# A fixed least time per DMA packet in the scheduler's picture, and row normalisation for the GEGLU layers begun one step ahead of its finish

## The chip, the cores and the metric

The kernel runs on one core of a Trainium2 chip. The metric is the device time of one execution in microseconds; for the kernel before the change three runs gave a median of 1600.6 us. Engines are named as the profile names them: PE (matmuls), PEld (its weight loads), DVE (elementwise), ACT (activations), POOL (GpSimd), SP (which issues most of the DMAs). "SPq" and "POOLq" are DMA issues on those queues.

## The reference, cut to what matters

The input is one sequence of 2048 rows with 512 columns in float32. Four layers alternate: a Fourier mixing layer (matrices for the hidden and the sequence direction, real part kept) and a GEGLU layer of width 1792. Each layer normalises the rows first and adds its result to the row.

```
def _A_ref(x, dft_seq_re, dft_seq_im, dft_hid_re, dft_hid_im):
    a = jnp.einsum("bsd,ed->bse", x, dft_hid_re)
    b = jnp.einsum("bsd,ed->bse", x, dft_hid_im)
    return jnp.einsum("ts,bse->bte", dft_seq_re, a) - jnp.einsum("ts,bse->bte", dft_seq_im, b)

def _B_ref(x, w_gate, w_up, w_down):
    return (_gelu(x @ w_gate) * (x @ w_up)) @ w_down

x = A_x
x = x + _A_ref(_layernorm(x, axis=-1), A_dft_seq_re, A_dft_seq_im, A_dft_hid_re, A_dft_hid_im)
x = x + _B_ref(_layernorm(x, axis=-1), B_w_gate, B_w_up, B_w_down)
x = x + _A_ref(_layernorm(x, axis=-1), A_dft_seq_re, A_dft_seq_im, A_dft_hid_re, A_dft_hid_im)
x = x + _B_ref(_layernorm(x, axis=-1), B_w_gate, B_w_up, B_w_down)
```

## The kernel before, in words

**Products.** Every float32 operand is split into a high and a low part of a shorter format. ACT writes the high part as a rounded copy (L121), DVE the low part as source minus high part (L123). A product is then three matmuls (`mm3`: L161 high by high, L162 high by low, L163 low by high), each with 128x128 weights and 512 moving columns, accumulated in one of eight PSUM banks. Larger products are done by blocks with seven instead of eight block products (the names A11, S1 to S4, T1 to T4, B11 and so on), which costs sums and differences on DVE (L149, L152) and copies out of PSUM on ACT (L156).

**Stages.** The layers follow each other: mixing layer 0 (`mix`, four blocks of 512 rows), GEGLU layer 1 in two halves of 1024 rows (`geglu`, w = 0 and 1), mixing layer 2, GEGLU layer 3 in two halves. SBUF is handed out in 93 slots of 128x512 (`sb.get`, `sb.put`). Two larger tiles, `wide` and `xwide`, hold four slots' width each; `load_turned` brings a group of 512 rows into one of them by four DMAs whose pieces are 512 bytes long (L229).

**Rows for a GEGLU layer.** `block_steps` prepares 1024 normalised rows as eight tiles of 128 rows. For each tile `norm(i)` starts the loads of the tiles that come next (`x_load_mixed`, four DMAs of 64 KB, L198), normalises its own tile (`normed`), turns it in 32x32 squares into its quarter of `wide` (DVE, L624) and, after each fourth tile, stores `wide` to DRAM (POOL's queue, L627). Later `fetch` reads it back by columns (L638, pieces of 512 bytes).

**Normalisation.** For the layers after the first, `norm_terms` needs ACT, POOL and ACT again, in this order: sum of the row (L518), mean (L519), sum of squares (L520) on ACT; add and power on POOL (L521, L522); shift on ACT (L523). `normed` then writes the normalised tile on ACT (L540). ACT's two passes over the row (L518, L520) must write their 512 columns somewhere, though only the sums are used: in `normed` they go into the tile `z` that later takes the result, in `terms_ahead` (which makes only the two terms, for mixing layer 2) into the one tile `junk`.

**What sets the order.** Python writes the steps in one order: a list `queue` that gives a step after each product, a list `slow` of which every ninth step takes one (`PACE`), and `chores` spread over the products of a mixing layer. For the first half of the rows of a GEGLU layer the steps of `block_steps` are chores of the mixing layer; for the second half they are in `slow` during w = 0. Then a scheduler reorders the instructions of each engine by a simulated time. The numbers of that picture are set in `machine_as_traced`: among them 3000 ns for an SP DMA to start, and 21.5 bytes per ns for each DMA engine. Each engine executes its own list strictly in order, so an ACT instruction that waits holds all that stand behind it.

Of the kernel before, what the change touches and what calls it, by code (L numbers as in the profile page):

```python
# [9 lines left out]
F32 = mybir.dt.float32  # L10
# [4 lines left out]
P = 128  # L15
# [6 lines left out]
NT = TB // P  # L22
# [28 lines left out]
SP_DELAY_NS = 3000  # L51
DEPTH = 1
DMA_BYTES_PER_NS = 21.5


@with_exitstack
def fnet_geglu(ctx: ExitStack, tc: tile.TileContext, x_in, ws, wh, whc, wgu, wdc, out):
# [468 lines left out]
    def terms_ahead(layer, i, n):  # L526
# [6 lines left out]
        known[layer, i] = norm_terms(layer, i, x, junk)  # L533
        sb.put(x)

    def normed(layer, i, mixed=False):
        x = row_of(layer, i, mixed)
        z = sb.get()
        rstd, shift = known.pop((layer, i), None) or norm_terms(layer, i, x, z)
        nc.scalar.activation(z, x, AF.Identity, bias=shift, scale=rstd)  # L540
        sb.put(x)
        return z
# [63 lines left out]
    def block_steps(layer, w):  # L606

        zt, t, wide = {}, {}, {}
        turned = [dram.tile([P, NT * D], F32, name=f"t{layer}_{w}_{part}") for part in range(2)]

        def norm(i):

            def run():
                r0 = w * 2 * NT
                end = 2 * NT if w else i // NT * NT + NT
                for k in range(i if i == 0 or i + NT == end and not w else i + 2, min(i + 3, end)):
                    fresh["mixed", r0 + k] = x_load_mixed(layer, r0 + k)
                z = normed(layer, r0 + i, True)
                part, n = divmod(i, NT)
                if n == 0:  # L620
                    assert not sb.out("z")
                    wide[part] = tpool.tile([P, NT * D], F32, name="wide")
                to = wide[part].rearrange("p (b n t) -> p b n t", n=NT, t=32)
                nc.vector.transpose(to[:, :, n], z.rearrange("p (b t) -> p b t", t=32))  # L624
                sb.put(z)
                if n == NT - 1:
                    nc.gpsimd.dma_start(turned[part], wide.pop(part))  # L627
# [25 lines left out]

        def second(c):
            def run():
                v = zt.pop((c, 1))
                if c < 2:
                    t["B12", c] = v
                    t["T1", c] = difference(v, t["B11", c])
                    sb.put(t.pop(("B11", c)))  # L660
                else:
                    c0 = c - 2
                    t["T2", c0] = difference(v, t["T1", c0])
                    t["T3", c0] = difference(v, t["B12", c0])
                    sb.put(t.pop(("B12", c0)))
                    blocks["B22", c0] = split_slot(v)
                    sb.put(v)
            return run

        def fourth(c):  # L670
            def run():
                t["T4", c] = difference(t["B21", c], t["T2", c])
                sb.put(t.pop(("B21", c)))
            return run

        def divide(name, c):
            def run():
                blocks[name, c] = split_slot(t[name, c])
                sb.put(t.pop((name, c)))
            return run  # L680

        one = [norm(i) for i in range(2 * NT)]
        two = [fetch(c) for c in range(ND)] + [first(c) for c in range(ND)] + [second(c) for c in range(ND)]
        two += [fourth(c) for c in range(2)]
        two += [divide(name, c) for name in ("T2", "T3", "T1", "T4") for c in range(2)]
        return one, two
# [690 lines left out]
def machine_as_traced():  # L1377
# [1 line left out]
    from concourse import hw_specs  # L1379

    spec = hw_specs.TRN2Spec
    kept = {name: getattr(spec, name) for name in ("PE_FULL_CLOCK_PASS_GAP_NS", "DGE_DMA_DELAY", "ENG_ISSUE_QUEUE_DEPTH", "DMA_BUS_BYTES_PER_NS_PER_ENGINE")}
    spec.PE_FULL_CLOCK_PASS_GAP_NS = PASS_GAP_NS
    spec.DGE_DMA_DELAY = {**spec.DGE_DMA_DELAY, mybir.EngineType.SP: SP_DELAY_NS}
    spec.DMA_BUS_BYTES_PER_NS_PER_ENGINE = DMA_BYTES_PER_NS
    depth = {mybir.EngineType.DVE: DEPTH, mybir.EngineType.Activation: DEPTH}
    spec.ENG_ISSUE_QUEUE_DEPTH = {**spec.ENG_ISSUE_QUEUE_DEPTH, **depth}
    try:
# [51 lines left out]
```

## Time and profile before

| | |
|---|---|
| runs | 1600.6 us median (1600.12 to 1602.94, 3 runs) |
| the profiled execution | 1600.54 us |
| its span, first to last instruction | 1598.8 us |
| TensorE clock | 0.999 of full speed |
| busy | PE 1586.9 us, DVE 1236.8, ACT 856.4, POOL 225.2 |
| matmuls | 7026, in three groups of 2334 and 24 short ones ahead |

A line of the trace gives start, duration, engine, line of the kernel, operation, output and inputs (buffer numbers left out) and count; behind it, in brackets, stands how long the engine was idle before it and what ended that. A matmul's duration (0.39 us) is longer than the distance to the next one, since matmuls overlap; the distance is what counts.

### The profile page before, as it was taken

How to read it: one execution, taken by the hardware profiler on the slowest of the kernel's cores; microseconds unless marked ns; L12 is line 12 of the kernel's file. 1: busy time of each engine (PE TensorE's matmuls, PEld its weight loads, DVE VectorE, ACT ScalarE, POOL GpSimd, SP SyncE). 2: the span in 40 equal slices, each digit the busy share in tenths (PEclk: the TensorE clock that was granted, in tenths of full speed). 3: DMA queues.
4: the chain of work that ended last, by engine and by line, in shares of the span. 5: the costliest groups of instructions: out<-in, count | busy, mean ns of one | idle time of the engine just before them, and what ended most of it. 6: DMA issues, size and time to landing. Idle time of an engine off the chain costs nothing.

```text
span 1598.8 us, 23017 instructions
## 1 busy us (share of the span) xinstructions
PE 1586.9 (99%) x7026; PEld 1313.1 (82%) x7026; DVE 1236.8 (77%) x2148; ACT 856.4 (54%) x1680; POOL 225.2 (14%) x410
## 2 busy tenths in 40 slices
PE   9999999999999999999999999999999999999998
PEld 7888788888878888788888888888888888888887
DVE  8999879789789795665869988789985548754484
ACT  7864454545666653556777435436446545433361
POOL 2212200112465201220041000001001000000000
PEclk9999999999999999999999999999999999999999
DMA  9949987787989899995967677778998967897462
GB/s 362 329 158 331 352 273 254 234 285 265 339 321 332 296 311 308 292 363 180 305 229 247 239 267 244 251 248 240 266 328 237 293 207 234 295 257 227 133 191 54
DMA packets 276379, 422.85 MB, mean 264 GB/s; under 512 B 28864, under 2 KB 131264, under 8 KB 275232
## 3 DMA queue, kind: packets, MB, share of 16 engines
q1 hardware_dynamic: 251600, 338.26, 67.0%
q0 software_dynamic: 23840, 82.73, 14.1%
q8 instruction: 56, 0.92, 0.2%
q14 instruction: 67, 0.55, 0.1%
q10 hardware_dynamic: 816, 0.39, 0.1%
HBM read 339.74 MB, written 81.53 MB: 263 GB/s over the span
## 4 chain that ended last, share of the span: by engine, by line
PE 83%; issue 12%; DMA 3%; ACT 1%; POOL 1%; DVE 0%; SPq 0%; POOLq 0%; ACTq 0%; DVEq 0%
PE p L162 28%; PE p L161 28%; PE p L163 28%; DMA s<-ws 2%; POOL rstd L521 0%; DMA wide<-x 0%; DMA s<-x 0%; ACT s L121 0%; DMA s<-wdc 0%; SPq L293 0%; ACT s L540 0%; DVE s L123 0%; DVE s L152 0%; POOL out L242 0%; ACT s L156 0%
## 5 line engine op out<-in xcount | busy, mean ns | idle before, releaser
L162 PE MATMUL p<-s,s 128*128 128x512 f32 (+1 forms) x2334 | 903.2, 388 | 1.1 <-DVE s L123 1.1
L163 PE MATMUL p<-s,s 128*128 128x512 f32 (+1 forms) x2334 | 891.9, 388 | 0.0
L161 PE MATMUL p<-s,s 128*128 128x512 f32 (+1 forms) x2334 | 874.9, 388 | 2.0 <-ACT s L156 1.5
L121 ACT ACTIVATE s<-s 128x512 fp32r<-128x512 f32 (+1 forms) x834 | 467.6, 607 | 344.4 <-DVE s L149 125.3
L123 DVE TENSOR_TENSOR s<-s,s 128x512 fp32r<-128x512 f32 (+1 forms) x834 | 521.2, 660 | 56.1 <-ACT s L121 53.9
L161 PEld LDWEIGHTS p<-s,s 128*128 128x128 f32 x2334 | 438.2, 188 | 94.6 <-ACT s L121 2.4
L162 PEld LDWEIGHTS p<-s,s 128*128 128x128 f32 x2334 | 438.4, 188 | 92.4 <-DVE s L123 2.6
L163 PEld LDWEIGHTS p<-s,s 128*128 128x128 f32 x2334 | 438.2, 188 | 89.7
L152 DVE TENSOR_TENSOR s<-s,p 128x512 f32<-128x512 f32 x290 | 194.8, 682 | 197.8 <-PE p L163 114.1
L149 DVE TENSOR_TENSOR s<-s,s 128x512 f32<-128x512 f32 (+1 forms) x403 | 242.3, 617 | 7.2 <-DMA s<-ws 4.9
L156 ACT ACTIVATE s<-p 128x512 f32<-128x512 f32 x246 | 143.8, 592 | 142.2 <-PE p L163 141.3
L1035 ACT ACTIVATE s<-s 128x512 f32<-128x512 f32 x112 | 70.1, 629 | 120.8 <-DVE s L152 120.1
L521 POOL TENSOR_SCALAR rstd<-rstd 128x1 f32<-128x1 f32 x48 | 18.6, 387 | 356.7 <-ACT s L520 271.3
L1049 DVE TENSOR_TENSOR s<-s,s 128x512 f32<-128x512 f32 x84 | 57.8, 688 | 1.7
L276 POOL DMA_DIRECT2D wb<-s x84 | 45.5, 544 | 88.7 <-ACT s L121 64.0
L121 ACT ACTIVATE s<-xwide 128x512 fp32r<-128x512 f32 (+1 forms) x66 | 39.8, 615 | 27.8 <-DVE xwide L149 14.6
L152 DVE TENSOR_TENSOR s<-s,s 128x512 f32<-128x512 f32 (+1 forms) x69 | 40.2, 586 | 15.6 <-DMA s<-ws 6.1
L540 ACT ACTIVATE s<-s,shift,rstd 128x512 f32<-128x512 f32 x59 | 47.6, 810 | 4.6 <-DVE shift L512 4.0
L123 DVE TENSOR_TENSOR s<-xwide,s 128x512 fp32r<-128x512 f32 (+1 forms) x66 | 44.0, 673 | 4.0 <-ACT s L121 3.1
L242 POOL DMA_DIRECT2D out<-wide x8 | 5.2, 655 | 287.1 <-DVE wide L152 182.2
L242 POOL DMA_DIRECT2D x<-wide x12 | 7.8, 659 | 234.1 <-DVE wide L152 234.1
L624 DVE STREAM_TRANSPOSE wide<-s 128x512 f32<-128x512 f32 x31 | 21.8, 705 | 20.3 <-ACT s L540 17.6
(121 smaller groups left out, 520.7 us busy)
## 6 DMA issues: line engine op xcount, KB each, us to landing
s<-ws SPq DMA_DIRECT2D x361, 256.0 KB, 5.1
s<-wb SPq DMA_DIRECT2D x294, 256.0 KB, 5.5
s<-wc SPq DMA_DIRECT2D x196, 256.0 KB, 4.8
wb<-s POOLq DMA_DIRECT2D x98, 256.0 KB, 5.8
s<-wh SPq DMA_DIRECT2D x85, 256.0 KB, 5.0
xwide<-ws SPq DMA_DIRECT2D x55, 256.0 KB, 4.5
s<-x SPq DMA_DIRECT2D x54, 256.0 KB, 4.5
wc<-s POOLq DMA_DIRECT2D x49, 256.0 KB, 6.0
```

Of the source, the lines that this page charges most:

```text
L121: nc.scalar.activation(hi, src, AF.Copy)
L123: nc.vector.tensor_tensor(lo, src, f32(hi), op=ALU.subtract)
L149: nc.vector.tensor_tensor(out, a, b, op=ALU.subtract)
L152: nc.vector.tensor_tensor(out, a, b, op=ALU.add)
L156: nc.scalar.activation(v, src, AF.Copy)
L161: nc.tensor.matmul(ps, ah, bh, start=start, stop=False, skip_group_check=True)
L162: nc.tensor.matmul(ps, ah, bl, start=False, stop=False, skip_group_check=True)
L163: nc.tensor.matmul(ps, al, bh, start=False, stop=stop, skip_group_check=True)
L276: nc.gpsimd.dma_start(a, f32(t))
L540: nc.scalar.activation(z, x, AF.Identity, bias=shift, scale=rstd)
L1035: nc.scalar.activation(t, g, AF.Gelu_apprx_tanh)
L1049: nc.vector.tensor_tensor(t, t, v, op=ALU.mult)
```

## The change

Two things change. First, the scheduler's picture gets a least time of 37 ns for each DMA packet (`DMA_MIN_TRANSFER_TIME`), beside the 21.5 bytes per ns; nothing of this is in the program itself, only the order that comes out of it. Second, in `block_steps` a step `norm(i)` only begins its tile (`norm_begun`: load and `norm_terms`, with `junk` as scratch), and `turn(i - 1)` finishes the one before (scale, transpose, store). One more step at the end finishes the last tile. All other callers of `normed` begin and finish at once, with `junk` as scratch too.

```
+DMA_PACKET_NS = 37
...
+    begun = {}
+    def norm_begun(layer, i, mixed=False):
+        x = row_of(layer, i, mixed)
+        begun[layer, i] = x, known.pop((layer, i), None) or norm_terms(layer, i, x, junk)
     def normed(layer, i, mixed=False):
-        x = row_of(layer, i, mixed)
+        if (layer, i) not in begun:
+            norm_begun(layer, i, mixed)
+        x, (rstd, shift) = begun.pop((layer, i))
         z = sb.get()
-        rstd, shift = known.pop((layer, i), None) or norm_terms(layer, i, x, z)
         nc.scalar.activation(z, x, AF.Identity, bias=shift, scale=rstd)
...
-                z = normed(layer, r0 + i, True)
...
+                norm_begun(layer, r0 + i, True)
+                if i:
+                    turn(i - 1)
             return run
+        def turn(i):
+            z = normed(layer, w * 2 * NT + i, True)
+            part, n = divmod(i, NT)
+            if n == 0:
+                wide[part] = tpool.tile([P, NT * D], F32, name="wide")
+            nc.vector.transpose(to[:, :, n], z.rearrange("p (b t) -> p b t", t=32))
+            sb.put(z)
+            if n == NT - 1:
+                nc.gpsimd.dma_start(turned[part], wide.pop(part))
...
-        one = [norm(i) for i in range(2 * NT)]
+        one = [norm(i) for i in range(2 * NT)] + [lambda: turn(2 * NT - 1)]
...
+    spec.DMA_MIN_TRANSFER_TIME = DMA_PACKET_NS
```

The program has the same instructions on each engine as before; only their order differs. Lines of the changed kernel are 1 higher up to L533 (L121 is L122, L156 is L157, L518 to L523 are L519 to L524), L540 is L549, and from the mixing layer on they are 15 higher (L973 is L988, L1025 is L1040, L1035 is L1050).

The first place is ACT at the normalisation of the sixth of the eight row tiles of the second half for GEGLU layer 1 (input `s0_5211`), before:

```order
L520 ACTIVATE s11_5559,rstd_5560<-s0_5211,mean_5563 128x512
L519 ACTIVATE mean_5734<-total_5733 128x1
L156 ACTIVATE s81_5517<-p4_5504 128x512
L121 ACTIVATE s72_5476<-s80_5311 128x512
L520 ACTIVATE s90_5730,rstd_5731<-s33_5385,mean_5734 128x512
L121 ACTIVATE s86_5608<-s52_5320 128x512
L523 ACTIVATE shift_5561<-mean_5563,rstd_5560 128x1
L121 ACTIVATE s6_5632<-s91_5321 128x512
L540 ACTIVATE s11_5559<-s0_5211,shift_5561,rstd_5560 128x512
L156 ACTIVATE s74_5499<-p0_5488 128x512
```

The same tile in the changed kernel:

```order
L519 ACTIVATE junk_86,total_5560<-s0_5211 128x512
L157 ACTIVATE s80_5235<-p0_5204 128x512
L122 ACTIVATE s72_5461<-s88_5174 128x256
L520 ACTIVATE mean_5561<-total_5560 128x1
L521 ACTIVATE junk_86,rstd_5558<-s0_5211,mean_5561 128x512
L122 ACTIVATE s85_5411<-s6_5171 128x512
L122 ACTIVATE s46_5441<-s29_5173 128x512
L524 ACTIVATE shift_5559<-mean_5561,rstd_5558 128x1
L1050 ACTIVATE s3_5268<-s80_5235 128x512
L157 ACTIVATE s28_5338<-p2_5240 128x512
L122 ACTIVATE s80_5368<-s37_5070 128x256
L122 ACTIVATE s26_5340<-s4_5162 128x512
```

The shift of this tile (L523, now L524) moved 25 rows forward on ACT, from row 521 to row 496. The PSUM copy that stands three rows behind it before (`s74_5499<-p0_5488`) is row 524 in both kernels, so 28 rows behind that shift now. In front of other work the shift stands now: the GELU `s3_5268`, the copy `s28_5338` and the split `s26_5340`, which is the eighth row further back than it was.

The second place is ACT in the other half (w = 1), where `terms_ahead` makes the terms of the rows of mixing layer 2; `s44_7578` is a row tile of it. Before:

```order
L156 ACTIVATE s55_7534<-p4_7456 128x512
L518 ACTIVATE junk_86,total_7742<-s44_7578 128x512
L519 ACTIVATE mean_7743<-total_7742 128x1
L520 ACTIVATE junk_86,rstd_7740<-s44_7578,mean_7743 128x512
L121 ACTIVATE s90_7536<-s70_7409 128x512
L518 ACTIVATE junk_86,total_7926<-s34_7738 128x512
L121 ACTIVATE s22_7659<-s85_7625 128x512
```

In the changed kernel this tile is `s59_7581`, and the two splits are `s12_7539<-s70_7412` and `s22_7662<-s84_7628`:

```order
L122 ACTIVATE s12_7539<-s70_7412 128x512
L157 ACTIVATE s73_7537<-p4_7459 128x512
L122 ACTIVATE s22_7662<-s84_7628 128x512
L519 ACTIVATE junk_86,total_7745<-s59_7581 128x512
L520 ACTIVATE mean_7746<-total_7745 128x1
L521 ACTIVATE junk_86,rstd_7743<-s59_7581,mean_7746 128x512
```

Both splits that stood behind the row's first pass now stand ahead of it.

The third place is SP at the load of that row tile (`s44_7578<-x2_1_94`, the last but one row shown), before:

```order
L229 DMA xwide_8470<-x1_2_91 32x16x128 x3
L1025 DMA s46_7607<-wb8_128 128x512
L1025 DMA s53_7608<-wb8_128 128x512
L1025 DMA s59_7596<-wb7_127 128x512
L1025 DMA s30_7621<-wb7_127 128x512
L973 DMA s85_7625<-whc 128x512
L229 DMA xwide_8470<-x1_2_91 32x16x128
L189 DMA s34_7738<-x2_1_94 128x512
L1025 DMA s7_7572<-wb7_127 128x512
L1025 DMA s4_7573<-wb7_127 128x512
L189 DMA s44_7578<-x2_1_94 128x512
L1025 DMA s64_7620<-wb7_127 128x512
```

And in the changed kernel (`s59_7581<-x2_1_94`):

```order
L988 DMA s84_7628<-whc 128x512
L190 DMA s59_7581<-x2_1_94 128x512
L230 DMA xwide_8473<-x1_2_91 32x16x128 x4
L989 DMA s28_7630<-whc 128x256
L990 DMA s27_7631<-whc 128x256
L190 DMA s89_7741<-x2_1_94 128x512
```

The load of the row now stands ahead of all four DMAs into `xwide` and directly behind the load from `whc`; before, all four were ahead of it.

At the beginning and at the end the rows are the same in both kernels: SP's first different row is the DMA that the trace before has at 193.76 us, PE's first different row is the matmul at 208.93 us, and PE's last different row is a matmul at 1391.00 us.

More of the change, by code (lines that the diff above doesn't have):

```diff
@@ L617, in run @@
                     fresh["mixed", r0 + k] = x_load_mixed(layer, r0 + k)
-                z = normed(layer, r0 + i, True)
[L619 to L627, printed above, removed]
-            return run
+                norm_begun(layer, r0 + i, True)
+                if i:
+                    turn(i - 1)
+            return run
+        def turn(i):
+            z = normed(layer, w * 2 * NT + i, True)
+            part, n = divmod(i, NT)
+            if n == 0:
+                assert not sb.out("z")
+                wide[part] = tpool.tile([P, NT * D], F32, name="wide")
+            to = wide[part].rearrange("p (b n t) -> p b n t", n=NT, t=32)
+            nc.vector.transpose(to[:, :, n], z.rearrange("p (b t) -> p b t", t=32))
+            sb.put(z)
+            if n == NT - 1:
+                nc.gpsimd.dma_start(turned[part], wide.pop(part))
         def fetch(c):
@@ L1381, in machine_as_traced @@
     spec = hw_specs.TRN2Spec
-    kept = {name: getattr(spec, name) for name in ("PE_FULL_CLOCK_PASS_GAP_NS", "DGE_DMA_DELAY", "ENG_ISSUE_QUEUE_DEPTH", "DMA_BUS_BYTES_PER_NS_PER_ENGINE")}
+    kept = {name: getattr(spec, name) for name in ("PE_FULL_CLOCK_PASS_GAP_NS", "DGE_DMA_DELAY", "ENG_ISSUE_QUEUE_DEPTH", "DMA_BUS_BYTES_PER_NS_PER_ENGINE", "DMA_MIN_TRANSFER_TIME")}
     spec.PE_FULL_CLOCK_PASS_GAP_NS = PASS_GAP_NS
```

## Prediction

> **What bounds the kernel now.** I read the page first, then the waits of PE, then PE's busy time in six stretches that I cut around its waits.
>
> ```profile
> span 1598.8 us, 23017 instructions
> PE 1586.9 (99%) x7026; PEld 1313.1 (82%) x7026; DVE 1236.8 (77%) x2148; ACT 856.4 (54%) x1680; POOL 225.2 (14%) x410
> PEclk9999999999999999999999999999999999999999
> ```
>
> PE is busy for 99% of the span and its clock is granted in full throughout. A change of order adds and removes no matmul, so it can only move the last per cent, and the question is where PE stands still.
>
> ```profile
> PE p L161 <- ACT s L156: 1.5, 2, 1.1
> PE p L1298 <- POOL ident masks.py:199: 1.4, 1, 1.4
> PE p L162 <- DVE s L123: 1.1, 2, 0.8
> PE p L161 <- ACT s L121: 0.5, 2, 0.3
> ...
> 0.00:193.00 193.00, 190.28 (x831) 156.47 (x832) 178.96 (x369) 123.88 (x228) 41.92 (x75) 1.00 0.87 307
> 193.00:470.00 277.00, 277.00 (x1224) 229.37 (x1223) 232.84 (x406) 151.97 (x312) 58.79 (x109) 1.00 0.85 283
> 470.00:490.00 20.00, 18.95 (x83) 15.33 (x83) 17.69 (x35) 14.87 (x34) 14.69 (x20) 1.00 0.81 285
> 490.00:655.00 165.00, 165.00 (x729) 136.64 (x728) 124.75 (x210) 91.29 (x185) 32.88 (x63) 1.00 0.97 308
> 655.00:675.00 20.00, 19.31 (x83) 14.93 (x82) 11.61 (x21) 11.45 (x28) 5.57 (x11) 1.00 0.85 275
> 675.00:1591.00 916.00, 916.00 (x4081) 760.16 (x4080) 670.09 (x1109) 462.91 (x897) 70.77 (x131) 1.00 0.77 242
> ```
>
> The columns are stretch, length, then busy us with count for PE, PEld, DVE, ACT, POOL, then clock, DMA share and GB/s. PE waits 4.5 us in all, in a few places. Behind 193 us there are only two stretches where PE is not busy throughout, 470 to 490 and 655 to 675; the other three have no idle time at all. In them a matmul begins every 277.00 / 1224 = 0.226 us. What is ahead of 193 us (the start, and one disturbance near 187 us) has the same rows in the same order in both kernels and stays. So does the end, where PE's last different row lies 200 us before the last matmul. Only the two bubbles can go.
>
> **What the two bubbles cost.** These are PE's rows around the first and the second.
>
> ```profile
> 477.76 0.39 PE L163 MATMUL p<-s,s 128*128 128x512 f32 x1
> 479.20 0.50 PE L161 MATMUL p<-s,s 128*128 128x512 f32 x1 [1.05 <-ACT s L156]
> 479.53 0.40 PE L162 MATMUL p<-s,s 128*128 128x512 f32 x1
> ...
> 662.50 0.61 PE L163 MATMUL p<-s,s 128*128 128x512 f32 x2
> ...
> 668.48 0.50 PE L161 MATMUL p<-s,s 128*128 128x512 f32 x1 [0.47 <-ACT s L156]
> 668.82 0.39 PE L162 MATMUL p<-s,s 128*128 128x512 f32 x1
> ```
>
> First: from 477.76 to 479.53 two distances take 1.77 us in place of 0.45, which is 1.32 us lost. Second: from 662.50 to 668.82 there are 21 distances, 6.32 us in place of 21 x 0.226 = 4.75, which is 1.57 us lost. Together **2.89 us**.
>
> **The first bubble: the order takes its cause away.** ACT, POOL and DVE around it:
>
> ```profile
> 473.36 0.62 ACT L121 ACTIVATE s<-s 128x512 fp32r<-128x512 f32 x1
> 477.14 0.29 ACT L523 ACTIVATE shift<-mean,rstd 128x1 f32<-128x1 f32 x1 [3.17 <-POOL rstd L522]
> 478.57 0.57 ACT L156 ACTIVATE s<-p 128x512 f32<-128x512 f32 x1
> ...
> 471.74 4.72 POOL L521 TENSOR_SCALAR rstd<-rstd 128x1 f32<-128x1 f32 x1
> ...
> 471.79 0.68 DVE L149 TENSOR_TENSOR s<-s,s 128x512 f32<-128x512 f32 x1
> ...
> 475.40 1.01 DVE L149 TENSOR_TENSOR s<-s,s 128x256 f32<-128x256 f32 x2
> ...
> L521 POOL TENSOR_SCALAR rstd<-rstd x48: 181/190/4725, 215.6 to 1280.7; 128x1 f32<-128x1 f32 x48
> L523 ACT ACTIVATE shift<-mean,rstd x48: 276/284/297, 217.2 to 1282.7; 128x1 f32<-128x1 f32 x48
> POOL rstd L522: 10.1, 11
> ```
>
> One of 48 POOL instructions at L521 takes 4.72 us in place of 0.19, over exactly the unbroken run of DVE instructions with two inputs in SBUF from 471.79 to 476.41. ACT's shift stands 3.17 us for it, and the PSUM copy three rows behind, for which PE waits until 479.20, comes late. The Trainium skill, SBUF — State Buffer, section Who interferes with whom, says that a DVE instruction with two SBUF inputs contends with a GpSimd instruction that reads SBUF, and that the second one blocks; by that rule the hold belongs to the neighbourhood and not to the row, and can come again wherever the row is put. The trace agrees, with the 4.72 us above. In the changed order this tile's shift stands 28 rows ahead of that copy, so the copy no longer hangs on it; the next tile's shift stands six rows ahead of it. Gain 1.32 us, if no other row takes the place.
>
> **What is late next there.** The shift now stands in front of a split whose traced times are these, with the matmul (second of three) that takes it:
>
> ```profile
> 456.53 1.15 ACT L121 ACTIVATE s<-s 128x512 fp32r<-128x512 f32 x2 [0.41 <-DVE s L1049]
> 460.99 0.84 PE L161 MATMUL p<-s,s 128*128 128x512 f32 x3
> ```
>
> The split ended near 457.15 and was taken at 461.21, about 4.1 us later. It stands eight ACT rows further back; two such rows take 1.15 us less an overlap, so a row is 0.5 to 0.6 us and eight are 4.0 to 4.8. The reserve is just about used up: 0 lost at best, 0.7 at worst, plus whatever POOL holds the shift. I book 0.2.
>
> **The second bubble: two changes of order.** ACT, then SP:
>
> ```profile
> 654.99 0.60 ACT L156 ACTIVATE s<-p 128x512 f32<-128x512 f32 x1
> 660.94 0.63 ACT L518 ACTIVATE junk<-s 128x512 f32<-128x512 f32 x1 [5.35 <-DMA s<-x]
> 662.65 0.61 ACT L121 ACTIVATE s<-s 128x512 fp32r<-128x512 f32 x1
> ...
> 648.90 0.33 SPq L973 DMA_DIRECT2D s<-whc  x1
> 649.90 0.32 SPq L229 DMA_DIRECT2D xwide<-x  x1
> 654.80 0.32 SPq L189 DMA_DIRECT2D s<-x  x1
> ```
>
> ACT stands 5.35 us for a row that SP issued at 654.80, and the splits that PE needs at 663 us are behind it. In the changed order the row is SP's next issue behind the one from `whc`, which was at 648.90; the next place was 649.90, so it goes 4.9 us earlier, and with the same 6.1 us of travel it lands at 656.0 in place of 660.9. Besides, both splits stand ahead of the row's first pass. Either alone ends the wait of 5.35 us as far as PE sees it. Gain 1.57 us. What is late next is the load that went behind: the four DMAs into `xwide` bring rows for a sum that comes at the end of this half, and nothing waited for them here.
>
> **The other edits.** `junk` in place of `z` as scratch costs nothing: the pass L518 takes 623 ns with either, and a tile of its own adds no wait since only ACT writes it.
>
> ```profile
> L518 ACT ACTIVATE s<-s 128x512 f32<-128x512 f32 x36 | 22.4, 623 | 22.2 <-DMA s<-x 18.7 <-PE p L162 1.9 <-issue 1.0
> L518 ACT ACTIVATE junk<-s 128x512 f32<-128x512 f32 x8 | 5.0, 623 | 5.4 <-DMA s<-x 5.3
> ```
>
> Finishing one step later moves L540, the transpose and the eight stores of `wide` back; PE reads those columns only at the next half or layer, so I book 0, and at worst a fetch comes late by a step of nine products (between 0 and about 2 us at 560 us, where DMA is full, below). Beginning earlier moves ACT's first pass towards its row's landing; those waits exist already (18.7 us in the row above) and of them PE saw only the one counted. The moved loads transfer the same bytes. The one stretch where that matters:
>
> ```profile
> 540.00:560.00 20.00, 20.00 (x90) 16.57 (x89) 15.43 (x26) 15.36 (x28) 0.00 (x0) 1.00 0.73 208
> 560.00:585.00 25.00, 25.00 (x112) 20.67 (x112) 24.93 (x42) 13.10 (x25) 0.00 (x0) 1.00 1.06 367
> ```
>
> From 560 to 585 us the DMA engines are full (share 1.06) while PE does not wait; a PE that arrives 1.32 us earlier eats that much of the weights' lead. I book 0.1 of a possible 1.32.
>
> **Sum.** Profiled execution 1600.54 (span 1598.8 and 1.7 around it; the median of the runs is 1600.6) - 1.32 - 1.57 + 0.2 + 0.1 = 1597.95, so **1598.0 us**, 0.16% below the median. A measurement of this kernel tells about 0.2%, or 3.2 us, from no change: 1597.4 to 1603.8 counts as the same.
>
> **The rivals.**
> 1. *The gain is given back.* A late shift at 458 to 462 us, or full DMA engines at 560 us, take 1 to 3 us again. For it: both reserves above are used up by the hand count. Against it: in the trace these very waits cost PE something in two of many places only. 1600.54 - 2.89 + 2 = 1599.7.
> 2. *Slower: POOL is held where ACT has no reserve.* The place is the opening of mixing layer 2, where PE needs the last normalised rows. The trace has the split there and its matmul:
>
> ```profile
> 845.46 1.96 DVE L123 TENSOR_TENSOR s<-s,s 128x512 fp32r<-128x512 f32 x4
> 852.67 0.39 PE L163 MATMUL p<-s,s 128*128 128x512 f32 x1
> ```
>
> The split (the second of four, ended near 846.5) had 6.2 us to spare; in the changed order ACT's part of it stands 7 rows later, some 3.6 to 4.2 us, so 2 to 2.6 are left. A hold of POOL as at 471.74 costs 4.5 us more than usual, and both POOL steps of a row (L521, L522) can be held: 9.0 - 2.6 = 6.4 us, 1597.65 + 6.4 = 1604.1. It decides from a hold of 2.6 us, and turns the sign from 5.5. This is also what the rule of the skill quoted above would do, since the change adds nothing against the hold. Against it: 1 hold of 48 over 2 us.
> 3. *The change does nothing where it counts*: the scheduler's picture is still wrong by more than it was moved, and the same waits stay. 1600.5. The order speaks against it at both places.
>
> **How the numbers follow.** Forecast 0.60, rival 1 0.22, rival 2 0.12, rival 3 0.06. The forecast spans 1597.2 to 1598.7 (runs scatter by some tenths; no more than the 2.89 can be gained, but the measured reference may lie a little higher), rival 1 up to 1600.6. The range of 1596.9 to 1601.5 leaves rival 2 and a little of the rest out. Faster by over 0.2% needs the whole 2.89 and 0.3 of scatter: 0.22, all from the forecast. Slower: 0.10, from rival 2. Same: 0.68.
>
> **What would show it.** Right: PE without idle time from 470 to 490 and from 655 to 675 us; ACT's wait of 5.35 us for the row gone and SP's row issued ahead of the `xwide` loads; the copy that PE waited for no longer behind a shift. Wrong: PE waits for ACT at 455 to 465 us or for a DMA at 555 to 575 us (rival 1), a POOL L521 of several us with PE idle near 850 us (rival 2), or the same two bubbles (rival 3). The prediction fails as a whole if PE waits in many small pieces behind 193 us where it had none.

## The result and the profile after

The changed kernel takes 1598.53 us in the median of 13 runs (1596.58 to 1599.92), the kernel before 1602.00 in 13 runs beside it (1600.02 to 1603.95). The ratio is 0.9974, 95% interval 0.9966 to 0.9981: 3.0 to 5.4 us less. The profiled execution took 1598.59 us. The head of its page, where the 54 instructions more than before are semaphore instructions alone:

```profile
span 1596.7 us, 23071 instructions
PE 1585.5 (99%) x7026; PEld 1311.8 (82%) x7026; DVE 1236.2 (77%) x2148; ACT 857.0 (54%) x1680; POOL 222.3 (14%) x410
```

The first in the list of PE's waits (us in all, times, longest); all four lie ahead of 193 us:

```profile
PE p L162 <- ACT s L122: 1.4, 4, 0.5
```

And PE's busy time in the stretches of the prediction, columns as there:

```profile
0.00:193.00 193.00, 188.89 (x827) 154.04 (x828) 178.02 (x368) 122.80 (x226) 42.05 (x75) 1.00 0.86 305
193.00:470.00 277.00, 277.00 (x1224) 229.33 (x1223) 232.00 (x402) 156.60 (x321) 59.16 (x112) 1.00 0.85 282
470.00:490.00 20.00, 20.00 (x90) 16.57 (x89) 19.47 (x39) 14.96 (x32) 12.04 (x23) 1.00 0.91 320
655.00:675.00 20.00, 20.00 (x90) 16.57 (x89) 13.36 (x23) 12.06 (x28) 5.88 (x11) 1.00 0.94 327
```

Both bubbles are gone: 20.00 of 20 us in each stretch, where 18.95 and 19.31 stood. The copy (L156, now L157) is no longer among what PE waits for. The stretch ahead of 193 us has the same rows in the same order, yet it lost more this time: 827 matmuls began in it instead of 831, which is 4 x 0.227 = 0.9 us. So the two profiled spans differ by 2.89 - 0.9 = 2.0 us, and by their own numbers by 1598.8 - 1596.7 = 2.1.

At the first place ACT's rows for the shift and for the copy are now these:

```profile
455.28 0.28 ACT L524 ACTIVATE shift<-mean,rstd 128x1 f32<-128x1 f32 x1
475.14 0.60 ACT L157 ACTIVATE s<-p 128x512 f32<-128x512 f32 x1 [0.76 <-PE p L164]
```

The shift is done 20 us ahead of the copy, and the copy waits for PE instead of PE for the copy. At the second place the timeline of ACT and of SP now reads:

```profile
656.11 0.63 ACT L122 ACTIVATE s<-s 128x512 fp32r<-128x512 f32 x1 [0.82 <-DVE s L1064]
...
657.13 0.62 ACT L122 ACTIVATE s<-s 128x512 fp32r<-128x512 f32 x1
657.65 0.62 ACT L519 ACTIVATE junk<-s 128x512 f32<-128x512 f32 x1
...
643.26 0.33 SPq L988 DMA_DIRECT2D s<-whc  x1
643.91 0.32 SPq L190 DMA_DIRECT2D s<-x  x1
644.51 2.79 SPq L230 DMA_DIRECT2D xwide<-x  x4
```

SP issues the row ahead of the four `xwide` loads, at 643.91 instead of 654.80. Both splits (L122) begin ahead of the row's pass (L519), which waits for nothing.

### The profile page after: what moved, and what is told of

Its sections match the earlier page's. It is cut to its first block, busy times and chain, and to the rows that moved or that the text cites. A ratio compares the mean times of both kernels' runs of the same rounds, so it can differ in the third digit from the quotient of the medians.

```text
span 1596.7 us, 23071 instructions
## 1 busy us (share of the span) xinstructions
PE 1585.5 (99%) x7026; PEld 1311.8 (82%) x7026; DVE 1236.2 (77%) x2148; ACT 857.0 (54%) x1680; POOL 222.3 (14%) x410
## 4 chain that ended last, share of the span: by engine, by line
PE 94%; DMA 2%; issue 1%; DVE 1%; POOL 1%; SPq 0%; ACT 0%; POOLq 0%; DVEq 0%; ACTq 0%
PE p L163 31%; PE p L162 31%; PE p L164 31%; DMA s<-ws 2%; DMA wc<-s 0%; POOL wh L277 0%; DVE s L124 0%; DMA s<-x 0%; ACT s L122 0%; DVE s L153 0%; POOL wc L277 0%; DVE s L150 0%; SPq L294 0%; SPq L190 0%; POOL out L1255 0%
## 5 line engine op out<-in xcount | busy, mean ns | idle before, releaser
L122 ACT ACTIVATE s<-s 128x512 fp32r<-128x512 f32 (+1 forms) x839 | 470.9, 607 | 337.9 <-DVE s L150 111.3
L124 DVE TENSOR_TENSOR s<-s,s 128x512 fp32r<-128x512 f32 (+1 forms) x839 | 526.6, 660 | 66.6 <-ACT s L122 54.4
L150 DVE TENSOR_TENSOR s<-s,s 128x512 f32<-128x512 f32 (+1 forms) x411 | 246.5, 615 | 9.1 <-DMA s<-ws 3.8
L157 ACT ACTIVATE s<-p 128x512 f32<-128x512 f32 x246 | 143.6, 593 | 149.7 <-PE p L164 145.3
L1050 ACT ACTIVATE s<-s 128x512 f32<-128x512 f32 x112 | 70.2, 629 | 118.9 <-DVE s L153 115.7
L122 ACT ACTIVATE s<-xwide 128x512 fp32r<-128x512 f32 (+1 forms) x61 | 36.7, 615 | 25.7 <-DVE xwide L150 7.9
L153 DVE TENSOR_TENSOR s<-s,s 128x512 f32<-128x512 f32 (+1 forms) x73 | 42.8, 590 | 8.3 <-DMA s<-ws 6.8
L549 ACT ACTIVATE s<-s,shift,rstd 128x512 f32<-128x512 f32 x58 | 46.2, 807 | 4.2 <-DVE shift L513 4.1
L124 DVE TENSOR_TENSOR s<-xwide,s 128x512 fp32r<-128x512 f32 (+1 forms) x61 | 40.5, 674 | 2.5 <-ACT s L122 2.5
L519 ACT ACTIVATE junk<-s 128x512 f32<-128x512 f32 x43 | 26.8, 624 | 22.3 <-DMA s<-x 21.9
```

What stands on the lines that cost most here:

```text
L122: nc.scalar.activation(hi, src, AF.Copy)
L124: nc.vector.tensor_tensor(lo, src, f32(hi), op=ALU.subtract)
L150: nc.vector.tensor_tensor(out, a, b, op=ALU.subtract)
L153: nc.vector.tensor_tensor(out, a, b, op=ALU.add)
L157: nc.scalar.activation(v, src, AF.Copy)
L1050: nc.scalar.activation(t, g, AF.Gelu_apprx_tanh)
```

## The experiments

All times are medians. "PE idle" names the places behind 193 us where the profile of that kernel shows PE waiting; single waits under 0.2 us are left out.

| kernel | us | before beside it | ratio (95%) | PE idle behind 193 us |
|---|---|---|---|---|
| full change | 1598.53 | 1602.00 | 0.9974 (0.9966 to 0.9981) | none |
| packet time alone | 1599.02 | 1602.10 | 0.9978 (0.9969 to 0.9987) | none |
| begun ahead alone | 1604.20 | 1602.10 | 1.0014 (1.0002 to 1.0027) | 662 to 667, 1259 us |
| `junk` alone | 1608.03 | 1602.10 | 1.0035 (1.0023 to 1.0048) | 445 to 452, 664, 1262 us |
| rows two ahead | 1601.54 | 1602.10 | 0.9991 (0.9981 to 1.0000) | 479, 654 us |
| packet time and `junk` | 1600.33 | 1602.68 | 0.9982 (0.9972 to 0.9991) | 448 us |
| begun ahead, mixed rows earlier | 1602.58 | 1602.68 | 0.9995 (0.9984 to 1.0005) | 449, 662 to 668, 1249 us |
| full, 27 ns | 1601.55 | 1602.68 | 0.9995 (0.9986 to 1.0004) | 667, 1264 us |
| full, 42 ns | 1602.80 | 1601.72 | 1.0006 (0.9996 to 1.0016) | 719, 850, 1352 us |
| full, 60 ns | 1628.82 | 1602.68 | 1.0159 (1.0145 to 1.0174) | many, below |

The theory was that of the prediction: two bubbles with one cause each, PE-bound otherwise. Its rivals were that both parts are needed, that any new order does it, and that the bubbles were chance.

**The packet time alone.** The kernel before with the constant and the line that sets it. In the trace of before, the 46848 packets of 512 bytes took 37 ns in the mean and 27 in the median.

```
+DMA_PACKET_NS = 37
...
+    spec.DMA_MIN_TRANSFER_TIME = DMA_PACKET_NS
```

> Only the first part of the change: the least time of 37 ns per DMA packet in the scheduler's picture. In this order the row s44_7578 is issued ahead of the xwide loads and both splits stand ahead of its first pass, as in the full change; the shift of the sixth row tile still stands three rows ahead of the copy that PE waited for. Theory (two bubbles, each with its own cause): PE without idle time from 655 to 675 us, the wait of about 1.3 us near 479 us still there; 1.6 us less than before in time, 1602.0 - 1.6 = 1600.4 by the medians so far, ratio 0.9990. Rival (the POOL hold of 4.72 us was one chance event of that one execution): no wait near 479 us either, 2.9 us less than before. Rival (gain from elsewhere, both parts needed together): no difference, or the bubble near 662 us still there.

It takes 3.1 us less than before, by the interval 2.1 to 5.0: more than the 1.6 of the theory. POOL and ACT at the first place, from the timeline:

```profile
474.02 3.52 POOL L522 TENSOR_SCALAR rstd<-rstd 128x1 f32<-128x1 f32 x1
...
478.20 0.29 ACT L524 ACTIVATE shift<-mean,rstd 128x1 f32<-128x1 f32 x1 [2.57 <-POOL rstd L523]
479.11 0.57 ACT L157 ACTIVATE s<-p 128x512 f32<-128x512 f32 x1
```

The two stretches of the bubbles:

```profile
470.00:490.00 20.00, 20.00 (x90) 16.52 (x89) 17.61 (x35) 15.19 (x36) 14.10 (x22) 1.00 0.87 294
655.00:675.00 20.00, 20.00 (x90) 16.58 (x89) 13.43 (x24) 12.17 (x28) 5.66 (x11) 1.00 0.87 277
```

The second bubble is gone, as expected. The hold of POOL and ACT's wait are still there, yet PE does not wait. It came to this place 1.98 us later than before (matmul number 2071 starts at 475.88, before at 473.90), because it had lost more ahead of 193 us. Whether that hid the bubble is the question of a second profile.

> The least packet time alone, profiled a second time. In the first profile POOL was held for 3.52 us at 474 us, ACT's shift stood 2.57 us, and yet PE did not wait: it came there 1.98 us later than before because of a longer wait at 185 us. Theory (the late opening hid it): if PE arrives 1 us or more earlier than in that first profile, it waits 0.3 to 1 us near 479 us; if it arrives as late, not. Rival (this order has reserve of its own there): no wait, however early PE arrives.

```profile
472.79 0.77 POOL L522 TENSOR_SCALAR rstd<-rstd 128x1 f32<-128x1 f32 x1
```

Matmul number 2071 starts at 474.65 here, 1.23 us earlier than in the first profile, and PE did not wait either. But the same POOL instruction was held for 0.77 us only, so the early PE did not meet a long hold, and this run by itself does not decide. The two traces together do: POOL's step begins 1.86 us ahead of matmul 2071 in both (in both profiles of before 2.16), so it moves with PE, and a late opening hides nothing. What saved the first profile is a hold of 3.52 in place of 4.72 us: the copy ended at 479.68, only 0.28 us ahead of the matmul that stood for it before (number 2089, at 479.96). By these numbers a hold of 4.72 us would have made PE wait some 0.9 us here too; that is an estimate. In this order the hold itself changes from one execution to the next. The execution took 1598.45 us, with no idle time of PE behind 193 us.

**The second part alone.** The changed kernel without the line that sets the least packet time:

```
-    spec.DMA_MIN_TRANSFER_TIME = DMA_PACKET_NS
```

> Only the second part of the change: normalisation begun one step ahead, own scratch tile. In this order the shift of the sixth row tile stands 28 rows further forward on ACT, 31 rows ahead of the copy; at the row s44_7578 rows of ACT and SP stand as before (row behind the xwide loads, splits behind the row's first pass). Theory: no wait near 479 us, the bubble of about 1.6 us between 660 and 669 us still there; 1.3 us less than before, 1600.7 by the medians so far, ratio 0.9992. Rival (packet time does it all): the wait near 479 us still there. Rival (gain given back): a new wait of 1 us or more between 455 and 470 us.

Both places came out as expected (no wait at 479 us, 19.33 of 20 us busy from 655 to 675), but the kernel is 2.1 us slower than before, by the interval 0.3 to 4.3, where 1.3 us less was expected. The loss is at a place that neither theory nor rival named: the last row tile of the second half for GEGLU layer 3. ACT and then PE, from the timeline:

```profile
1258.61 0.63 ACT L519 ACTIVATE junk<-s 128x512 f32<-128x512 f32 x1 [5.63 <-DMA s<-x]
...
1260.70 0.57 ACT L157 ACTIVATE s<-p 128x512 f32<-128x512 f32 x1
...
1258.98 0.39 PE L164 MATMUL p<-s,s 128*128 128x512 f32 x1
1261.33 0.50 PE L162 MATMUL p<-s,s 128*128 128x512 f32 x1 [1.96 <-ACT s L157]
...
1262.74 0.63 PE L164 MATMUL p<-s,s 128*128 128x512 f32 x1
...
1265.72 0.44 PE L162 MATMUL p<-s,s 128*128 128x512 f32 x1
```

And PE's stretch behind the wait; the last three columns are the granted clock, the DMA share and GB/s:

```profile
1262.40:1265.60 3.20, 3.20 (x9) 2.52 (x8) 1.39 (x2) 0.64 (x2) 0.00 (x0) 0.50 1.03 373
```

ACT stands 5.63 us for a row, and the PSUM copy behind it (1260.70) is what PE waits for. PE then runs at half its clock for about 3.4 us, a matmul every 0.43 us. From 1258.98 to 1265.72 there are 13 distances, 6.74 us instead of 13 x 0.227 = 2.95: 3.8 us lost, 1.7 of it behind the wait itself. The ACT rows of this place, begun ahead alone and then the full change:

```
L157 ACTIVATE s_13880<-p_13873 128x512
L519 ACTIVATE junk,total<-s_14040 128x512
L520 ACTIVATE mean<-total 128x1
L1050 ACTIVATE s_13947<-s_13892 128x512
L521 ACTIVATE junk,rstd<-s_14040,mean 128x512
L157 ACTIVATE s_13966<-p_13885 128x512
```

```
L157 ACTIVATE s_13880<-p_13873 128x512
L1050 ACTIVATE s_13947<-s_13892 128x512
L157 ACTIVATE s_13966<-p_13885 128x512
L519 ACTIVATE junk,total<-s_14040 128x512
```

In the full change the same copy stands ahead of the same row. In the full change's timeline ACT waits for this row too, 3.88 us, but what PE needs next is already done:

```profile
1254.69 0.58 ACT L157 ACTIVATE s<-p 128x512 f32<-128x512 f32 x1
1259.15 0.63 ACT L519 ACTIVATE junk<-s 128x512 f32<-128x512 f32 x1 [3.88 <-DMA s<-x]
```

**The scratch tile alone.**

```
-        rstd, shift = known.pop((layer, i), None) or norm_terms(layer, i, x, z)
+        rstd, shift = known.pop((layer, i), None) or norm_terms(layer, i, x, junk)
```

> The kernel before with one word changed: the two passes of normed write into junk in place of z. In this order the shift of the sixth row tile stands 28 rows further forward too, though nothing is begun one step ahead. Theory: the scratch tile alone is what ends the wait near 479 us; bubble of about 1.6 us at 660 to 669 us stays, 1.3 us less than before, 1600.7. Rival (it is the split into begin and finish that does it): the wait near 479 us stays, no difference to before.

As expected, this one word ends the wait at 479 us: it moves the shift. But it costs 5.9 us by the medians. By the distances between matmuls 5.9 us are lost at the same place as above and another 1.6 at 445 to 452 us. ACT and PE at the first of these:

```profile
1263.38 0.63 ACT L518 ACTIVATE junk<-s 128x512 f32<-128x512 f32 x1 [7.56 <-DMA s<-x]
...
1266.23 0.65 PE L161 MATMUL p<-s,s 128*128 128x512 f32 x1 [4.03 <-ACT s L156]
```

The group of all these passes (busy us, mean ns | idle time ahead, and for what):

```profile
L518 ACT ACTIVATE junk<-s 128x512 f32<-128x512 f32 x45 | 28.0, 623 | 41.0 <-DMA s<-x 40.9
```

With `z` the pass stands at ACT row 1356, with `junk` at 1340, while the row's load stays SP's issue 1231. ACT's waits for rows in this group grow from 18.7 + 5.3 (the two groups of before) to 40.9 us. That `z` must be a free slot and `junk` need not would explain the shift; that is argued from the code, only the rows' places are shown.

**Rows two ahead.** The rows of `terms_ahead` are loaded two ahead, in the kernel before.

```
...
-        if i + 1 < n:
-            fresh["terms"] = x_load(layer, i + 1)
+        if i + 2 < n:
+            fresh["terms", i + 2] = x_load(layer, i + 2)
...
```

> The kernel before with one edit: the rows whose terms are made for mixing layer 2 are loaded two ahead in place of one. The load of s44_7578 stands 24 issues further forward on SP, the first bubble's rows as before. Theory (the second bubble is the late row and nothing else): ACT's wait of 5.35 us for a row at 655 to 661 us and PE's idle time from 655 to 675 us gone, the wait near 479 us still there; 1.6 us less than before, 1600.4. Rival (it is the splits' place on ACT, or full DMA engines, that costs the time at 662 us): PE still waits there for an ACT split, or for other loads that the earlier rows push back; same time as before or more.

The wait at 479 us is there again (1.07 us for the copy, POOL held for 4.73), so the first bubble repeats. The bubble at 662 us is gone, but the same wait came back earlier, at another row:

```profile
655.21 0.63 ACT L518 ACTIVATE junk<-s 128x512 f32<-128x512 f32 x1 [5.75 <-DMA s<-x]
655.84 0.58 ACT L156 ACTIVATE s<-p 128x512 f32<-128x512 f32 x1
...
656.47 0.50 PE L161 MATMUL p<-s,s 128*128 128x512 f32 x1 [2.23 <-ACT s L156]
```

The scheduler put the pass forward with the load. An earlier load did not help here, where the pass is placed by the same picture. The theory's time is missed; that a row's late landing, with a copy behind it, stops PE is confirmed.

**Packet time and scratch tile, nothing begun ahead.** The first experiment, with the one word of the third.

```
+DMA_PACKET_NS = 37
...
-        rstd, shift = known.pop((layer, i), None) or norm_terms(layer, i, x, z)
+        rstd, shift = known.pop((layer, i), None) or norm_terms(layer, i, x, junk)
```

> Least packet time of 37 ns and junk as scratch, but nothing begun one step ahead. In this order ACT's first pass over the last row tile for the second GEGLU layer is ACT row 1343 (1340 with junk alone, 1341 in the full change, 1356 before) and SP's load of it is issue 1231, as before. Theory (the scratch tile alone makes the scheduler put the pass 15 to 17 rows forward, towards a load that stays where it was; the packet time puts it back by the few rows that PE needs): no idle time of PE near 479, 662 or 1259 us, time as with the full change, 1598.5, ratio 0.9975. Rival (the split into begin and finish is needed beside the other two): PE waits near 1259 us as with junk alone, 3 to 6 us more than the full change.

No idle time at 479, 662 or 1259 us: the packet time does put the pass back as far as PE needs. But PE loses 1.0 us near 448 us, which neither theory nor rival had. ACT there, then POOL:

```profile
445.80 0.29 ACT L524 ACTIVATE shift<-mean,rstd 128x1 f32<-128x1 f32 x1 [2.44 <-POOL rstd L523]
...
444.57 0.60 POOL L628 DMA_DIRECT2D t<-wide  x1 [2.87 <-DVE s L124]
445.20 0.57 POOL L523 TENSOR_TENSOR rstd<-rstd,power 128x1 f32<-128x1 f32 x1
```

ACT's shift waits for a step that POOL has behind a store of `wide`, which itself waits for DVE. With the split into begin and finish this wait of PE is not there (277.00 of 277 us busy from 193 to 470). So the split may have a use beside `junk`; by the times this is not shown, since the intervals of this kernel and of the full change overlap.

**Begun ahead, with the mixed rows loaded one tile earlier.** The second part alone, with

```
-                for k in range(i if i == 0 or i + NT == end and not w else i + 2, min(i + 3, end)):
+                for k in range(i if i == 0 or i + NT == end and not w else i + 3, min(i + 4, end)):
```

> The second part alone (begun one step ahead, junk), and the mixed rows loaded one tile further ahead. The load of the last tile is SP issue 1220 in place of 1232, its first pass ACT row 1330 in place of 1339; at about 1 us per issue and per row the load goes some 12 us forward and the pass some 9. Theory (the 4.3 us that the second part alone loses between 1235 and 1266 us are the late landing of this row, with the PSUM copies behind it on ACT): ACT's wait of 5.6 us for the row shrinks to 2 to 3.5 us and PE's wait of 2 us with the nine slow matmuls behind it is gone; the bubble at 661 to 667 us stays; 1604.2 - 4.3 = 1599.9. Rival (the loss there is full DMA engines, share 1.08, and not the row): PE waits there all the same, time of the second part alone, 1604.

```profile
1247.77 0.63 ACT L519 ACTIVATE junk<-s 128x512 f32<-128x512 f32 x1 [5.47 <-DMA s<-x]
...
1250.67 0.73 PE L162 MATMUL p<-s,s 128*128 128x512 f32 x2 [1.08 <-ACT s L122]
```

A miss in part: ACT's wait did not shrink. The load's last issue went 12.4 us forward (1241.41 in place of 1253.78), but ACT came to the pass 10.7 us earlier, and from the last issue to the pass it took 6.4 in place of 4.8 us. PE waits 1.08 instead of 1.96 us, for another row behind it, and its clock stays full, so the loss there is 1.3 instead of 3.8 us. A new wait at 449 us takes 1.1 of it back. The rival is not excluded: PE still waits there, and from 1235 to 1266 us the DMA share is 1.09 here and 1.06 with the second part alone.

**The value of the packet time.** Full change with 27, 42 and 60 instead of 37 (at 21.5 bytes per ns 512 bytes take 24 ns and 1024 take 48, so by this arithmetic 60 also lengthens the packets of 1024 bytes, and the others do not):

```
-DMA_PACKET_NS = 37
+DMA_PACKET_NS = 27
```

> The full change with a least packet time of 27 ns in place of 37 (24 is what 512 bytes take at 21.5 bytes per ns). In this order the row for the terms (the second bubble's) is issued behind two of the four xwide loads, and the two splits stand behind its first pass, as before; at 479 and 1259 us rows stand as with 37. Theory: the second bubble is there (about 1.5 us at 655 to 670 us), the first not, nothing at 1259 us; 1.3 us less than before. Rival (any least time does it): PE without idle time behind 193 us, 3 us less than before.

> The full change with 42 ns in place of 37. At the places of the three bubbles ACT and SP stand as with 37 or later by one to three rows (last row tile's first pass at ACT row 1341 as with 37, the row for the terms ahead of all xwide loads, both splits ahead of its pass). Theory (each value is one order, and the loss with 60 ns comes from other rows): time as with 37, 1598.5 +- 1. Rival (the time grows with the value beyond 37, since 37 to 60 cost 30 us): 1603 to 1606.

> The full change with a least packet time of 60 ns in place of 37. In this order the row for the terms stands ahead of all xwide loads and one split ahead of its first pass, the other two rows ahead of it as well; the last row tile's first pass is ACT row 1346, five rows later than with 37. Theory (later passes, more reserve): none of the three bubbles, time as with 37, 1598.5. Rival (a longer time in the picture moves other loads too early or copies too late): a new wait of PE of 1 us or more where there was none.

With 27 ns the second bubble stays, as expected: ACT waits 5.34 us for the row, and PE 1.09 us for a copy. Near 1259 us nothing was expected, and PE waits 0.31 us at 1264.93.

```profile
661.24 0.63 ACT L519 ACTIVATE junk<-s 128x512 f32<-128x512 f32 x1 [5.34 <-DMA s<-x]
...
668.64 0.50 PE L162 MATMUL p<-s,s 128*128 128x512 f32 x1 [1.09 <-ACT s L157]
```

With 42 ns the forecast of no difference to 37 fails. Its largest loss is the prediction's second rival at its place, POOL first, then ACT, then PE:

```profile
845.82 3.10 POOL L522 TENSOR_SCALAR rstd<-rstd 128x1 f32<-128x1 f32 x1 [2.96 <-ACT junk L521]
...
849.58 0.29 ACT L524 ACTIVATE shift<-mean,rstd 128x1 f32<-128x1 f32 x1 [2.19 <-POOL rstd L523]
...
850.04 0.39 PE L164 MATMUL p<-s,s 128*128 128x512 f32 x1
853.01 0.79 PE L162 MATMUL p<-s,s 128*128 128x512 f32 x1 [2.58 <-ACT s L122]
...
856.15 0.40 PE L163 MATMUL p<-s,s 128*128 128x512 f32 x1
```

From 850.04 to 856.15 there are 8 distances: 6.11 us instead of 1.81, so 4.3 lost. This execution took 1604.03 us; the ten runs of this kernel lie between 1600.96 and 1604.96, and whether the hold comes in the shorter ones is not shown. With 60 ns the forecast of no loss fails by 30 us. PE loses in many places; the largest loss is at the opening of mixing layer 2 (stretch, columns as above):

```profile
850.00:885.00 35.00, 27.71 (x104) 21.06 (x104) 27.62 (x64) 35.00 (x90) 9.28 (x18) 0.90 0.45 142
```

ACT is busy for all of the 35 us (the fourth busy time; in the full change 22.61) and PE for 27.71. First in the list of PE's waits are those for ACT's splits, 11.0 us in six. So 37 is neither the beginning nor the middle of a plateau: 27 and 42 both lose the gain.

**The kernel before, profiled a second time.**

> The kernel before, unchanged, profiled a second time. Theory (the bubbles come with the order): PE waits again at 478 to 480 us for the copy (about 1.3 us lost, less if PE arrives there over 0.6 us later than in the first profile) and at 660 to 669 us (1.6 us), POOL is held for 4.7 us at 472 us. Rival (chance of one execution): one or both are absent with PE arriving at the same time.

SP, ACT and PE at the second bubble:

```profile
657.59 0.32 SPq L189 DMA_DIRECT2D s<-x  x1
...
663.53 0.63 ACT L518 ACTIVATE junk<-s 128x512 f32<-128x512 f32 x1 [8.93 <-DMA s<-x]
...
661.51 0.61 PE L163 MATMUL p<-s,s 128*128 128x512 f32 x2
665.90 1.06 PE L161 MATMUL p<-s,s 128*128 128x512 f32 x2 [3.78 <-ACT s L121]
...
669.69 0.39 PE L161 MATMUL p<-s,s 128*128 128x512 f32 x1
```

Both bubbles are there again. The first is the same (POOL held for 4.73 us, PE waits 1.05 for the copy). The second is much larger: SP issued the row at 657.59 instead of 654.80, ACT waited 8.93 instead of 5.35 us, and PE's clock fell to half behind the wait. Why SP issued it later is not shown. From 661.51 to 669.69 there are 11 distances, 8.18 us instead of 2.49: 5.7 us lost, against 1.57 in the first profile. This execution took 1603.68 us.

**The hold by itself.** A small kernel with twelve DVE instructions in each run: `both` is DVE adding two SBUF tiles, `psum` one from PSUM, `single` one input, `mixed` a PSUM input in every fourth place.

```
for i, op in enumerate(ops):
    op(c[i % 4])
    if i == 0:
        nc.scalar.activation(rstd, c[0][:, 0:1], AF.Copy)
        nc.gpsimd.tensor_scalar(rstd, rstd, 1.0 / D, EPS, op0=ALU.mult, op1=ALU.add)
```

> A small kernel that computes nothing of the reference (its output is one tile, sixteen times): a 128x1 TENSOR_SCALAR on POOL is released behind the first of twelve DVE instructions of 128x512, in four kinds, three times each. Theory (POOL is held by an unbroken run of DVE instructions with two inputs in SBUF, until the run ends): with two SBUF inputs it takes about 11 x 0.6 = 6.6 us; with the second input in PSUM or with one input 0.2 us; with a PSUM input in every fourth place it ends at the first of these, after some 1.2 to 1.9 us. Rival (any run of DVE instructions holds it, or none does and the 4.7 us were something else): the same time in all four.

The first turn of `both`, `psum` and `single` on POOL, and DVE's run beside the first:

```profile
5.66 0.34 POOL L86 TENSOR_SCALAR rstd<-rstd 128x1 f32<-128x1 f32 x1 [5.21 <-ACT rstd L85]
13.33 0.19 POOL L86 TENSOR_SCALAR rstd<-rstd 128x1 f32<-128x1 f32 x1 [7.34 <-ACT rstd L85]
20.63 0.34 POOL L86 TENSOR_SCALAR rstd<-rstd 128x1 f32<-128x1 f32 x1 [7.11 <-ACT rstd L85]
...
4.66 7.30 DVE L71 TENSOR_TENSOR both<-a,b 128x512 f32<-128x512 f32 x12
```

The theory falls: in an unbroken run of twelve DVE instructions with two SBUF inputs, POOL's takes 0.34, 0.28 and 0.27 us in the three turns, and is done within the run. The rival (the same in all four) holds no better: with a PSUM input it is 0.19 each time, with one input 0.34, and `mixed` 0.27 to 0.28. In each of the nine turns above 0.19 it ends 0.05 us after the end of the DVE instruction that ran when it began. The holds in the large kernels end the same way, but behind a whole run: in the 13 profiles 25 of the 624 steps of this kind take over 1 us, and each ends 0.05 us after the last of one or more DVE instructions that run on without a break and without a PSUM input. Yet of 154 steps with at least three such instructions ahead only 17 stood to the end of the run. So the run says where a hold ends, and not whether one comes. The distance to the next DVE instruction alone does not decide it either: holds of 4.7 us began 0.04 to 0.05 us ahead of it, one of 4.35 us (with 27 ns) 0.20 ahead, and the short steps of `both` 0.14 to 0.20 ahead.

## Why the prediction was right, point by point

**What bounds the kernel.** Right. PE is the bound, and what can go behind 193 us are its bubbles. Where a profile shows none (full change, packet time alone in both profiles), the spans differ by what was lost ahead of 193 us.

**First bubble, 1.32 us.** The size was right: it is the same in both profiles of before and with the rows two ahead. The step "this tile's shift stands 28 rows ahead of that copy, so the copy no longer hangs on it" was right: the scratch tile alone does it. But it was not the only way, since with the packet time alone the shift stays three rows ahead of the copy and PE does not wait either, in two profiles of two; in the first of them with 0.28 us to spare.

**Second bubble, 1.57 us.** The cause was right (row, splits, copies behind it), the size was that of one execution. A second one shows 5.7. So, by these two profiles, what the change removes lies between 1.3 + 1.6 and 1.3 + 5.7 us, and 3.5 was measured, above the 2.6 that the forecast takes from 1600.54. The row went forward more than counted: 10.9 us in place of 4.9. "Either alone ends the wait" is not shown. The load alone was moved with the rows two ahead, where its pass moved along and the wait came back at 654 us; with 27 ns neither the load nor the splits had moved far enough.

**The time.** 1598.53 lies 0.6 us from the 1597.95 of the sum, and part of that is luck. The reference of 1600.54 was 1.5 us below the median of before that was measured beside (1602.00; the later medians are 1601.7 to 1602.7), and the gain was counted 0.9 us too small. These two errors point opposite ways.

**"`junk` in place of `z` as scratch costs nothing" and "those waits exist already".** This step failed, though the sum hides it. The tile adds no wait of its own, as said; but it lets the scheduler place a pass 15 to 17 rows earlier, in front of copies, while the load stays. Alone it costs 5.9 us, with the split 2.1. The step counted the instruction's cost and its semaphores, not what the freed place does to the order at the other row tiles. The prediction looked at the places where PE waited before, and this one was not among them. In the full change the packet time takes it back.

**The two reserves, 0.2 and 0.1 us.** Nothing was lost at 458 to 462 us or from 560 to 585 us.

**Rivals.** The first one (gain given back) did not come in the full change; in kernels next to it the gain was given back at 448 and 1259 us, places that it had not named. The second one (POOL held at the opening of mixing layer 2) did not come with 37 ns, and came with 42 ns at its place, with a hold of 3.10 us. Its point of decision was given as 2.6 us of hold; beyond that it counted a hold's excess only, 0.3 us for this one, and 4.3 were lost, part of it at the half clock. The hold is not enough by itself either: with the packet time and `junk` a POOL step at this place was held for 3.13 us (at 845.50), and PE did not wait. The rule of the Trainium skill that the rival leaned on (SBUF — State Buffer, section Who interferes with whom) speaks of one instruction that blocks another, and the small kernel agrees with that: 0.27 to 0.34 in place of 0.19 us. The prediction took the 4.72 us as agreement too, but that hold spans eight DVE instructions, which the rule does not give. Why POOL stands for so many in some executions stays open.

**Which part brings the gain.** The packet time alone gives 3.1 us and the full change 3.5, which these intervals can't tell apart; the second part alone costs 2.1. No kernel here is measurably better than the full change. That any new order brings the gain is excluded: of the other orders here, 27 and 42 ns gain nothing that the intervals show, and the second part alone, `junk` alone and 60 ns lose.

## What to carry over

In a kernel whose engines execute their lists in order, a scratch buffer of its own is a change of order: look for which waiting instruction it lets move in front of others, at every repetition of the step and not only where the bound engine waits today. A correction of the scheduler's picture should be tried alone first, and at values on either side, since a neighbouring value may lose all that one value gains. A bubble that hangs on a DMA has a different size in each execution: read it from two profiles before it enters a sum.

## What the runs showed of the hardware

- **TensorE's clock falls to half after a short stop.** Stops between two matmuls of 2.35, 2.62, 2.97, 4.2 and 4.4 us were followed by about 3.4 us in which a matmul began every 0.43 us (granted clock 0.50 above); single stops of up to 2.19 us, as the one below in the packet time's first profile, were not. This roughly doubles the price of a wait of 2 to 3 us, by 1.6 us. Shorter stops close together did it too: with 60 ns one of 1.70 us was followed by the half clock, where another of 0.70 us had begun 1.04 us before.

```profile
185.07 0.39 PE L163 MATMUL p<-s,s 128*128 128x512 f32 x1
187.26 0.50 PE L163 MATMUL p<-s,s 128*128 128x512 f32 x1 [1.80 <-DVE s L124]
```

  The Trainium skill, TensorE: Matmul & The Clock Gate, section Why this matters for your kernels, asks for no gaps above about 3 us. Here 2.35 us from start to start (1.96 us idle) was already too long; the measurement decides.
- **The same instruction in the same order is held differently.** The POOL step at 474 us took 3.52 us in one execution and 0.77 in another; the one at 471 us took 4.72, 4.73 and 4.73 in the three profiles with the old order there (before twice, rows two ahead). In the prediction's rows the hold ended with a run of DVE instructions; the other long holds end so too, but such a run alone does not make one (17 of 154).
- **The opening scatters.** Ahead of 193 us, with the same rows, 823 to 835 matmuls began in five profiles (before twice, the full change, the packet time alone twice): up to 12 x 0.227 = 2.7 us between executions, near what the whole change is worth.
